# Sigmoid attention, routed experts and a SwiGLU-like layer on one core: operand pieces made inside the second layer and stored by the sync engine, first operands requested in tile 18, decodes and first casts at other places

## The chip, the cores and the metric

One core of one Trainium2 chip runs the whole kernel in one launch. The metric is the device time of one execution in microseconds (us); lower is better.

## The reference, cut to what matters

```python
scores = q @ k.T / sqrt(64) - log(448)            # 4 batches, 12 heads, 448 tokens
x = sigmoid(scores) @ v                           # -> 1792 tokens x 768
e = argmax(x @ w_gate)                            # one of 8 experts per token
y = gate * (relu(x @ w1[e]) @ w2[e])              # 768 -> 1024 -> 768
h = y @ w_in                                      # 768 -> 2048, w_in and w_out given as float64
out = (h * sigmoid(h)) @ w_out                    # 2048 -> 768
```

All results are float32. w_in and w_out arrive as 64-bit words, which the kernel turns into float32 itself.

## The kernel before

Every float32 matrix product is made of three products of rounded parts. An operand is cast to a high part (ScalarE, ACT) and the rest is subtracted out as a low part (VectorE, DVE); TensorE (PE) then adds high x high, high x low and low x high in PSUM. The names ending in h and l are those parts. The order on each engine is the order in which the code is written; each engine, and each queue that requests DMAs (that of the sync engine, SP, of ACT and of GpSimd, POOL), works strictly in that order.

**Stage 1, attention** (`scores`, `av`, `evac`, `xform`; steps k = 0 to 97, four per pair of heads, 24 pairs). `split_k` (in the first two steps of a pair) and `split_q` (in the last two) make the parts of the next pair's k and q. Beside it, `predecode` turns raw 64-bit words of w_in and of NO of the 16 w_out slabs into float32: `decode` is five DVE instructions of 128 x 768 with a yield after the second to fifth, `combine` forms the differences that the later seven-product scheme needs. The step loop draws from it with `next(pd, 0)`, six times in a pair. The last pair's loads, the first expert's weights and stores of decoded slabs leave from SP's queue.

**Stage 2, experts**: tiles t = 0 to 20 of 128 tokens sorted by expert. Some tiles from 7 to 13 are skipped by a branch. A tile is the first layer (`l1`, 36 matmuls of 128 x 512), `relu`, `htrans`, `xtrans` of the next tile, the second layer (`l2`, 48 matmuls of 128 x 384) and `yout` (ACT scales, SP stores to Yd). Where the next tile has another expert, a branch runs `split1` (six casts on ACT and six subtractions on DVE, of 128 x 1024) for its w1 and then loads the next; `split2` does so for w2, in the first layer and in the second. `early` decodes six more w_out slabs in tiles 1 and 2. In tile 0 the parts of w2 are made by `split2` in three calls.

**Between stages 2 and 3**, `xprep` makes the operands of the last layer: for a chunk c of 128 tokens it takes two gathered blocks of rows (`ra`, `rb`), transposes them in four groups of three (`tr`), forms sums and differences s1, s2, a21, s4, splits seven pieces into parts (`split(i, ...)`) and stores the 14 parts with `put` to T0 (first 1024 tokens, chunks 0 to 3, tiles 15 to 18) or T1 (other 768, chunks 0 to 2, in pass 0 of stage 3, `xprep1`). In stage 3 high parts, and the low parts of the first three pieces, lie in a ring of two buffers (tag `sl`), so a cast waits until an older part has landed in DRAM. `xload` brings the stored operands back: operands 0 and 1 are requested after tile 19, 2 to 4 in tile 20, 5 and 6 after it.

**Stage 3** (`ffn2`, pass 0 with 1024 tokens, pass 1 with 768; j = 0 to 7 in each). Each j makes seven products (63 matmuls of 128 x 512 in pass 0: the P phase), gates them (`gate`), and multiplies with w_out for the 8 (pass 1: 6) tiles of 128 tokens (96 or 72 matmuls of 128 x 384: the Y phase); DVE adds each tile to `acc`. Four PSUM buffers hold two tiles of y, so the third tile waits for the first tile's add. In pass 0 `bg(p)` draws one step of background work 12 times in a j, four of them in the P phase: first `wdecode`, the rest of w_out, one slab after the other through one raw buffer, then `xprep1`. In the last j of pass 0, between the P and the Y phase, these lines stand:

```python
if p == 0 and last:
    for _ in bgs:
        pass
    for i in range(7):
        xo[1][i] = xload(1, i)
```

Of the kernel before, what the change touches and what calls it, by code (L numbers as in the profile page):

```python
# [51 lines left out]
EARLY = {1: 3, 2: 3}  # L52
NO = 4
NM = NO + sum(EARLY.values())
# [12 lines left out]
def attn_moe_ffn(ctx: ExitStack, tc, qT, kT, v, wg, w1, w2, w_in, w_out, out):  # L67
# [604 lines left out]
    for k in range(0, G + LAG, 2):  # L672
# [25 lines left out]
        for j in (k, k + 1):  # L698
            background(j)
            if j >= 3:  # L700
                next(pd, 0)
                if j % 2:
                    next(pd, 0)
            if cur is None and j >= G - 8 and not tasks:
                cur = prep(0, (B - 1) * S)
                gg = gate(0, cur[1], (B - 1) * S)
            if j >= 4 * UG and j % 8 == 1 and TF + (j - 4 * UG) // 8 < TG:
                t = TF + (j - 4 * UG) // 8
                nc.sync.dma_start(out=Yd[t * 128:(t + 1) * 128], in_=zero)
# [37 lines left out]

    def split2(r, pool=(FC - 1,)):
        for k in r:
            nc.scalar.copy(out=w2h[:, k], in_=stage2[:, k])  # L750
            eng = nc.gpsimd if k in pool else nc.vector
            eng.tensor_sub(out=w2l[:, k], in0=stage2[:, k], in1=w2h[:, k])  # L752
# [54 lines left out]
    split2(range(0, 2), (1,))  # L807
    hs0 = relu(0, 0, ph0)
    until(x3, "pr")
    pn = counts()  # L810
# [6 lines left out]
    until(x3, "tt")  # L817
    split2(range(2, 4), (3,))
    nxt, nn = prep(1), prep(2)
# [8 lines left out]
    h1 = htrans(0, 1, hs1)  # L828
    split2(range(4, FC), (5, 7))
    until(tb, "ne")  # L830
# [18 lines left out]
    def xprep(p, c, ra, rb, tmp, slab, px, free=None):  # L849
# [4 lines left out]

        def put(i, ap, eng=nc.sync):
            eng.dma_start(out=td[i, :, :, cs], in_=ap.rearrange("p (k m) -> p k m", k=KH))

# [7 lines left out]
        def split(i, a, l=None):  # L865
            if free is None:
                h, s = slab()
                l = l if s is None else s
                nc.scalar.copy(out=h.bitcast(F32R), in_=a)
                nc.vector.tensor_sub(out=l.bitcast(F32R), in0=a, in1=h)  # L870
                put(2 * i, h, nc.scalar)
                put(2 * i + 1, l, nc.gpsimd)
                return
            h = slab()
            l = slab() if l is None else l
            nc.scalar.copy(out=h.bitcast(F32R), in_=a)
            put(2 * i, h)
            nc.vector.tensor_sub(out=l.bitcast(F32R), in0=a, in1=h)
            put(2 * i + 1, l)
# [63 lines left out]
    for t in range(TMAX):  # L943
# [10 lines left out]
        if t > 0:  # L954
# [23 lines left out]
            if t == TMAX - 1:  # L978
                M1.close()
                L0.close()  # L980
                F1 = Group("left")
                wp, xpa = F1.pool("f_w", 1), F1.pool("f_xa", 1)
                wiload(0)
                for i in (2, 3, 4):
                    xps[i] = xpa
                    xo[0][i] = xload(0, i)
                wops = [*wisplit()]
            l2(py, *h0, range(2, 4))
            l2(py, *h1, range(4, 8))
        if 0 < t and t + 1 < TMAX:  # L990
# [10 lines left out]
        yout(t, py, gg, tk)  # L1001
        if XPT <= t < XPT + NX:
            for _ in xg:
                pass
        if XPT - 1 <= t < XPT + NX - 1:
# [4 lines left out]
            if c == 0:  # L1010
# [6 lines left out]
                       (lambda it: lambda: next(it))(slabs), lambda i: keep(ps_t, [128, 384], F32, f"t{i}", 0))  # L1017
        if t == XPT + NX:
            for i in range(2):
# [46 lines left out]
    def wdecode():  # L1066
        raw = xs_t[:, 0:2 * DM].bitcast(I32).rearrange("p (n w) -> p n w", w=2)
        bt, sq = xs_t[:, 2 * DM:3 * DM].bitcast(I32), xs_t[:, 3 * DM:4 * DM]
        rawload(raw, w_out[:, NM], nc.sync)
        for f in range(NM, F2C):  # L1070
            yield 1
            yield 1
# [230 lines left out]
```

## Time and profile before

| | us |
|---|---|
| median of 3 runs (1079.37 to 1082.52) | 1081.44 |
| the profiled execution: time | 1077.8 |
| the profiled execution: span of the trace | 1076.1 |
| PE busy in the span | 1003.9 (93%) |
| DVE busy | 704.0 (65%) |
| ACT busy | 486.8 (45%) |
| POOL busy | 127.1 (12%) |

Times in the trace count from the start of the span. A busy PE is one on which a matmul is under way; it says nothing about the clock, which has a column of its own (1.00 is full speed).

### The profile page before, as it was taken

The page shows a single profiled execution, that of the slowest core. Times are in us where ns is not written, and L with a number is a line of the kernel's source. Part 1 is how long each engine was busy: PE and PEld are TensorE (multiplying, and loading weights), DVE is VectorE, ACT ScalarE, POOL GpSimd, SP SyncE. Part 2 cuts the span into 40 slices and gives each one's busy share as a digit, 9 for nine tenths or more (in the row PEclk, how much of TensorE's full clock was granted, in tenths as well). Part 3 has the DMA queues.
Part 4 walks back from the last instruction along what each step waited for, and adds up shares of the span by engine and source line. Part 5 has one row for each costly group of instructions (what it writes and reads, how often), then busy time and mean ns, then how long its engine had stood idle before and what let it go on. Part 6 is the DMA issues. An engine that isn't in the chain of part 4 may idle for free. (4 is left out here: it accounts for less than half of the span.)

```text
span 1076.1 us, 15547 instructions
## 1 busy us (share of the span) xinstructions
PE 1003.9 (93%) x5404; PEld 841.5 (78%) x5404; DVE 704.0 (65%) x1419; ACT 486.8 (45%) x823; POOL 127.1 (12%) x136
## 2 busy tenths in 40 slices
PE   7999998889999999898879879999999999999997
PEld 4555544579888998787768668898888899999997
DVE  5899994887775248363551337776876765777764
ACT  5666655421675246363442344322444336443342
POOL 1000000133122111224341000000000030000002
PEclk9999999999999999999989889999999999999999
DMA  8999999377698129597875933434454792222222
GB/s 287 332 328 316 323 311 272 122 248 257 251 344 324 33 89 357 175 329 207 266 262 188 416 133 125 169 125 134 127 176 159 263 380 83 81 82 82 81 81 89
DMA packets 83803, 226.12 MB, mean 210 GB/s; under 512 B 10176, under 2 KB 46528, under 8 KB 77696
## 3 DMA queue, kind: packets, MB, share of 16 engines
q1 hardware_dynamic: 63072, 188.02, 49.7%
q0 software_dynamic: 7584, 31.48, 8.7%
q10 hardware_dynamic: 13056, 5.51, 2.0%
q8 instruction: 44, 0.72, 0.3%
q14 instruction: 47, 0.39, 0.1%
HBM read 167.16 MB, written 57.82 MB: 209 GB/s over the span
## 5 line engine op out<-in xcount | busy, mean ns | idle before, releaser
L1197 PE MATMUL y<-wo,gl 128*128 128x384 f32 x448 | 151.6, 338 | 8.3 <-DVE gl L1130 8.3
L1195 PE MATMUL y<-wo,gh 128*128 128x384 f32 x448 | 152.1, 339 | 2.0 <-DVE acc L1206 2.0
L1196 PE MATMUL y<-wo,gh 128*128 128x384 f32 x448 | 150.6, 336 | 0.0
L1206 DVE TENSOR_TENSOR acc<-acc,y 128x384 f32<-128x384 f32 x196 | 101.3, 549 | 20.7 <-PE y L1197 20.4
L244 ACT ACTIVATE a<-s,bias 128x896 f32<-128x896 f32 x96 | 82.6, 911 | 68.5 <-PE s L241 68.4
L782 PE MATMUL y<-w2h,hh 128*128 128x384 f32 x304 | 105.6, 347 | 0.7 <-ACT hh L772 0.7
L783 PE MATMUL y<-w2l,hh 128*128 128x384 f32 x304 | 102.7, 338 | 3.3 <-POOL w2l L752 3.1
L784 PE MATMUL y<-w2h,hl 128*128 128x384 f32 x304 | 102.6, 337 | 0.9 <-DVE hl L773 0.9
L757 PE MATMUL h<-w1h,xh 128*128 128x512 f32 x228 | 93.8, 411 | 3.2 <-issue 2.0
L758 PE MATMUL h<-w1l,xh 128*128 128x512 f32 x228 | 92.7, 407 | 2.1 <-DVE w1l L746 1.5
L1197 PEld LDWEIGHTS y<-wo,gl 128*128 128x128 f32 x448 | 84.8, 189 | 10.3 <-DVE gl L1130 9.9
L759 PE MATMUL h<-w1h,xl 128*128 128x512 f32 x228 | 91.2, 400 | 0.0
L1195 PEld LDWEIGHTS y<-wo,gh 128*128 128x128 f32 x448 | 84.7, 189 | 4.7 <-DVE acc L1206 4.4
L1196 PEld LDWEIGHTS y<-wo,gh 128*128 128x128 f32 x448 | 84.7, 189 | 0.3
L773 DVE TENSOR_TENSOR hl<-x,hh 128x512 fp32r<-128x512 f32 x38 | 26.2, 689 | 89.0 <-ACT hh L772 66.2
L257 PE MATMUL o<-a,vf 128*64 128x448 f32 x384 | 84.0, 560 | 0.0
L935 DVE TENSOR_TENSOR wl<-wf,wh 128x384 fp32r<-128x384 f32 x112 | 60.7, 552 | 19.3 <-ACT wh L934 19.2
L1116 PE MATMUL X<-x,wh 128*128 128x512 f32 (+1 forms) x192 | 71.3, 371 | 1.3 <-ACT c L1156 1.3
L1117 PE MATMUL X<-x,wh 128*128 128x512 f32 (+1 forms) x192 | 70.3, 366 | 1.3 <-DMA x<-T 1.3
L1118 PE MATMUL X<-x,wl 128*128 128x512 f32 (+1 forms) x192 | 70.0, 365 | 0.0
L783 PEld LDWEIGHTS y<-w2l,hh 128*128 128x128 f32 x304 | 57.7, 190 | 4.0 <-POOL w2l L752 3.4
L1130 DVE TENSOR_TENSOR gl<-sg,gh 128x512 fp32r<-128x512 f32 (+1 forms) x64 | 40.0, 625 | 31.5 <-ACT gh L1128 30.4
(246 smaller groups left out, 2036.0 us busy)
## 6 DMA issues: line engine op xcount, KB each, us to landing
stage<-w SPq DMA_DIRECT2D x14, 1536.0 KB, 8.5
wf<-Wi SPq DMA_DIRECT2D x16, 1344.0 KB, 5.8
stage<-w SPq DMA_DIRECT2D x8, 1920.0 KB, 12.7
stage<-w_in SPq DMA_DIRECT2D x16, 768.0 KB, 6.4
wof<-Wo SPq DMA_DIRECT2D x16, 768.0 KB, 8.1
stage<-w SPq DMA_DIRECT2D x8, 1152.0 KB, 5.7
x<-T SPq DMA_DIRECT2D x12, 768.0 KB, 10.3
Yd<-ys SPq DMA_DIRECT2D x19, 384.5 KB, 4.7
```

The lines of the kernel that those rows point to most:

```text
L244: nc.scalar.activation(out=a[:, 0:n], in_=ps[:, 0:n, 0:S], func=AF.Sigmoid, bias=bias, scale=1.0 / math.sqrt(D))
L257: nc.tensor.matmul(out=po[pr][r, 0:S], lhsT=vf[:, g, r], rhs=a[:, i if n == 2 else 0], start=(g == 0), stop=(g == NG - 1))
L757: nc.tensor.matmul(out=ph, lhsT=xh[:, k], rhs=w1h[:, k, cs], start=(k == 0), stop=False)
L758: nc.tensor.matmul(out=ph, lhsT=xh[:, k], rhs=w1l[:, k, cs], start=False, stop=False)
L759: nc.tensor.matmul(out=ph, lhsT=xl[:, k], rhs=w1h[:, k, cs], start=False, stop=(k == KC - 1))
L782: nc.tensor.matmul(out=o, lhsT=hh[:, c], rhs=w2h[:, f, ys], start=(f == 0), stop=False)
L783: nc.tensor.matmul(out=o, lhsT=hh[:, c], rhs=w2l[:, f, ys], start=False, stop=False)
L784: nc.tensor.matmul(out=o, lhsT=hl[:, c], rhs=w2h[:, f, ys], start=False, stop=(f == FC - 1))
L1195: nc.tensor.matmul(out=o, lhsT=gh[:, cs], rhs=w_[:, f, 0, ys], start=st, stop=False)
L1196: nc.tensor.matmul(out=o, lhsT=gh[:, cs], rhs=w_[:, f, 1, ys], start=False, stop=False)
L1197: nc.tensor.matmul(out=o, lhsT=gl[:, cs], rhs=w_[:, f, 0, ys], start=False, stop=sp)
L1206: nc.vector.tensor_add(out=a, in0=a, in1=o)
```

## The change

`NO` falls from 4 to 2: two w_out slabs fewer are decoded in the attention stage and two more in pass 0, where `wdecode` now passes 13 steps before its first slab and takes six steps for a slab in place of seven. The steps that the attention loop draws are placed otherwise within a pair. In tile 0 the casts of w2 stand right after the first `relu`, and one subtraction goes from POOL to DVE. The four chunks of T0 are made between the matmuls of the second layer, not after the tile; all their stores leave from SP, and their last four subtractions go to POOL. `xload` of operands 0 and 1 stands after tile 18.

```diff
@@ -50,7 +50,7 @@
 KH = KC // 2
 HK = KH * 128
 EARLY = {1: 3, 2: 3}
-NO = 4
+NO = 2
 NM = NO + sum(EARLY.values())
 NL = TMAX - TMIN
 TF = TMIN - NL
@@ -699,7 +699,7 @@
             background(j)
             if j >= 3:
                 next(pd, 0)
-                if j % 2:
+                if j % NG >= 2:
                     next(pd, 0)
             if cur is None and j >= G - 8 and not tasks:
                 cur = prep(0, (B - 1) * S)
@@ -745,9 +745,10 @@
             nc.scalar.copy(out=w1h[:, k], in_=stage1[:, k])
             nc.vector.tensor_sub(out=w1l[:, k], in0=stage1[:, k], in1=w1h[:, k])
 
-    def split2(r, pool=(FC - 1,)):
+    def split2(r, pool=(FC - 1,), cast=True):
         for k in r:
-            nc.scalar.copy(out=w2h[:, k], in_=stage2[:, k])
+            if cast:
+                nc.scalar.copy(out=w2h[:, k], in_=stage2[:, k])
             eng = nc.gpsimd if k in pool else nc.vector
             eng.tensor_sub(out=w2l[:, k], in0=stage2[:, k], in1=w2h[:, k])
 
@@ -806,6 +807,8 @@
     l1(ph0, 0, *xhl, range(KC))
     split2(range(0, 2), (1,))
     hs0 = relu(0, 0, ph0)
+    for k in range(2, FC):
+        nc.scalar.copy(out=w2h[:, k], in_=stage2[:, k])
     until(x3, "pr")
     pn = counts()
     l1(ph1, 1, *xhl, range(KC))
@@ -815,7 +818,7 @@
     h0 = htrans(0, 0, hs0)
     hs1 = relu(0, 1, ph1)
     until(x3, "tt")
-    split2(range(2, 4), (3,))
+    split2(range(2, 4), (3,), False)
     nxt, nn = prep(1), prep(2)
     rawm = [ot_p[1].tile([128, DM, 2], I32, tag="ot", name="rawm0"),
             sqp[:, 0:2].rearrange("p n d -> p (n d)").bitcast(I32).rearrange("p (n w) -> p n w", w=2),
@@ -826,7 +829,7 @@
     py = psy(0)
     l2(py, *h0, range(0, 2))
     h1 = htrans(0, 1, hs1)
-    split2(range(4, FC), (5, 7))
+    split2(range(4, FC), (7,), False)
     until(tb, "ne")
     ne = ne1 = reg(tbl[0][0:1, 2, 0:1], (SP,), E - 1)
     nc.sync.dma_start(out=stage1, in_=wsrc(w1, ne, 0, KC))
@@ -852,8 +855,8 @@
         cs = slice(c * 128, (c + 1) * 128)
         td = T1 if p else T0
 
-        def put(i, ap, eng=nc.sync):
-            eng.dma_start(out=td[i, :, :, cs], in_=ap.rearrange("p (k m) -> p k m", k=KH))
+        def put(i, ap):
+            nc.sync.dma_start(out=td[i, :, :, cs], in_=ap.rearrange("p (k m) -> p k m", k=KH))
 
         def tr(rows, half, i):
             q = px(i)
@@ -865,11 +868,12 @@
         def split(i, a, l=None):
             if free is None:
                 h, s = slab()
+                eng = nc.gpsimd if s is None else nc.vector
                 l = l if s is None else s
                 nc.scalar.copy(out=h.bitcast(F32R), in_=a)
-                nc.vector.tensor_sub(out=l.bitcast(F32R), in0=a, in1=h)
-                put(2 * i, h, nc.scalar)
-                put(2 * i + 1, l, nc.gpsimd)
+                eng.tensor_sub(out=l.bitcast(F32R), in0=a, in1=h)
+                put(2 * i, h)
+                put(2 * i + 1, l)
                 return
             h = slab()
             l = slab() if l is None else l
@@ -985,8 +989,20 @@
                     xps[i] = xpa
                     xo[0][i] = xload(0, i)
                 wops = [*wisplit()]
+            px = xg if XPT <= t < XPT + NX else iter(())
+            next(px, 0)
+            next(px, 0)
             l2(py, *h0, range(2, 4))
-            l2(py, *h1, range(4, 8))
+            next(px, 0)
+            next(px, 0)
+            next(px, 0)
+            next(px, 0)
+            l2(py, *h1, range(4, 6))
+            next(px, 0)
+            next(px, 0)
+            l2(py, *h1, range(6, 8))
+            for _ in px:
+                pass
         if 0 < t and t + 1 < TMAX:
             i, c = entry(t + 1, late)
             fr = reg(tbl[i][0:1, 0, c], (ACT, DVE, SP, POOL), 1)
@@ -999,9 +1015,6 @@
         for _ in range(EARLY.get(t, 0)):
             early()
         yout(t, py, gg, tk)
-        if XPT <= t < XPT + NX:
-            for _ in xg:
-                pass
         if XPT - 1 <= t < XPT + NX - 1:
             c = t + 1 - XPT
             rows = ot_p[1].tile([128, 2, YW], F32, tag="ot", name=f"rows{c}")
@@ -1015,7 +1028,7 @@
                          [(sl8[:, 6], None), (sl8[:, 7], None), (rw[:, 0:HK], None), (rw[:, HK:2 * HK], None)])
             xg = xprep(0, c, rows[:, 0], rows[:, 1], [sl4[:, i] for i in range(4)],
                        (lambda it: lambda: next(it))(slabs), lambda i: keep(ps_t, [128, 384], F32, f"t{i}", 0))
-        if t == XPT + NX:
+        if t == XPT + NX - 1:
             for i in range(2):
                 xo[0][i] = xload(0, i)
         if t == 1:
@@ -1067,8 +1080,9 @@
         raw = xs_t[:, 0:2 * DM].bitcast(I32).rearrange("p (n w) -> p n w", w=2)
         bt, sq = xs_t[:, 2 * DM:3 * DM].bitcast(I32), xs_t[:, 3 * DM:4 * DM]
         rawload(raw, w_out[:, NM], nc.sync)
+        for _ in range(13):
+            yield 1
         for f in range(NM, F2C):
-            yield 1
             yield 1
             yield 1
             for i, _ in enumerate(decode(raw, sq, bt)):
```

Three places in the instruction order. First ACT in tile 17; `w2h` and `w1h` are expert weights, `t`, `sl`, `w` and `rows` hold xprep's pieces, `T` is the store to DRAM. Before:

```order
L750 CAST w2h<-stage_102 128x768 x3
L974 UNCONDITIONAL_BRANCH x2
L106 TENSOR_LOAD tbl_78
L994 COMPARE_AND_BRANCH
L745 CAST w1h<-stage_88 128x1024 x6
L994 UNCONDITIONAL_BRANCH x2
L795 ACTIVATE ys_2557<-y_2420,gg_2561 128x768
L885 COPY sl_5208<-t_0_2220 128x384
L869 CAST w_98<-t_0_2221 128x384
L856 DMA T_65<-w_98 384x1x128
L869 CAST w_98<-t_0_2220 128x384
L856 DMA T_65<-w_98 384x1x128
```

and after:

```order
L889 COPY sl_5194<-t_0_2206 128x384
L873 CAST w_98<-t_0_2207 128x384
L873 CAST w_98<-t_0_2206 128x384
L873 CAST w_98<-t_0_2207 128x384
L873 CAST w_98<-sl_5194 128x384 x2
L873 CAST rows_5650<-sl_5194 128x384 x2
L106 TENSOR_LOAD tbl_78
L1010 COMPARE_AND_BRANCH
L745 CAST w1h<-stage_88 128x1024 x6
L1010 UNCONDITIONAL_BRANCH x2
L796 ACTIVATE ys_2543<-y_2410,gg_2547 128x768
```

The pieces moved ahead of the six casts of w1 and of the output; the stores left ACT.

Second, POOL at the end of tile 16, where `rows` are the gathered rows of the next chunk, `gg` and `gx` gates and rows of coming tiles. Before:

```order
L856 DMA T_65<-w_98 384x1x128 x3
L856 DMA T_65<-sl_5208 384x1x128 x4
L843 DMA rows_5664<-Yd,cidx 128x769 x2
L590 DMA gg_2561<-Gd,gi_2400 128x1
L960 COMPARE_AND_BRANCH
L960 UNCONDITIONAL_BRANCH x2
L584 DMA gx_2402<-Xd,gi_2622 128x768
```

and after:

```order
L874 TENSOR_TENSOR sl_5194<-sl_5194,w_98 128x384 x2
L874 TENSOR_TENSOR sl_5194<-sl_5194,rows_5419 128x384 x2
L106 TENSOR_LOAD tbl_78
L1010 COMPARE_AND_BRANCH
L1010 UNCONDITIONAL_BRANCH x2
L846 DMA rows_5650<-Yd,cidx 128x769 x2
L590 DMA gg_2547<-Gd,gi_2390 128x1
L964 COMPARE_AND_BRANCH
L964 UNCONDITIONAL_BRANCH x2
L584 DMA gx_2392<-Xd,gi_2608 128x768
```

Seven stores on POOL became four subtractions, still ahead of the gathers.

Third, PE at the end of the P phase of the last j of pass 0 (X collects the last product, `ft` takes xprep1's transposes, y_7_4 is the Y phase's first tile). Before:

```order
L1116 MATMUL X<-x_6_6524,wh_6_8608 128x512
L1117 MATMUL X<-x_6_6524,wh_6_8608 128x512
L1118 MATMUL X<-x_6_6524,wl_6_8609 128x512
L1195 MATMUL y_7_4_0_8759<-wo_8643,gh_7_3_8698 128x384
L1196 MATMUL y_7_4_0_8759<-wo_8643,gh_7_3_8698 128x384
```

and after:

```order
L1130 MATMUL X<-x_6_6510,wh_6_8510 128x512
L1131 MATMUL X<-x_6_6510,wh_6_8510 128x512
L1132 MATMUL X<-x_6_6510,wl_6_8511 128x512
L864 MATMUL ft<-ident,xs_t 128x128 x12
L1209 MATMUL y_7_4_0_8759<-wo_8562,gh_7_3_8632 128x384
L1210 MATMUL y_7_4_0_8759<-wo_8562,gh_7_3_8632 128x384
```

Twelve transposes, a whole chunk of `xprep1`, now stand between the two phases. Before, the three chunks' transposes all stood in earlier phases.

## Rows read from the trace of the kernel before

**Rows 1.** The page, its first part: busy us, share, instructions of PE.

```profile
PE 1003.9 (93%) x5404; PEld 841.5 (78%) x5404; DVE 704.0 (65%) x1419; ACT 486.8 (45%) x823; POOL 127.1 (12%) x136
```

**Rows 2.** Waits of PE: releaser, us in total, times, longest.

```profile
PE x L769 <- ACT hs L763: 10.4, 5, 6.8
PE y L1197 <- DVE gl L1130: 8.3, 2, 7.7
PE s L241 <- DVE ql L223: 6.6, 10, 1.1
...
PE t L861 <- DVE sl L890: 4.3, 4, 1.6
PE t L861 <- ACT sl L885: 3.3, 4, 1.2
...
PE y L783 <- POOL w2l L752: 3.1, 1, 3.1
```

**Rows 3.** Stretches: length, busy us of each engine, PE's clock, DMA share, GB/s.

```profile
20.00:160.00 140.00, 133.38 (x817) 72.26 (x819) 127.39 (x316) 88.18 (x132) 0.00 (x0) 1.00 0.97 318
459.40:580.20 120.80, 103.23 (x540) 90.39 (x539) 60.08 (x113) 53.52 (x91) 41.68 (x46) 0.94 0.76 248
542.60:547.30 4.70, 4.70 (x13) 3.76 (x14) 1.66 (x3) 0.58 (x1) 3.62 (x3) 0.50 0.62 195
560.40:580.20 19.80, 18.53 (x101) 16.47 (x100) 6.92 (x14) 5.66 (x11) 6.65 (x9) 1.00 0.55 162
584.00:614.00 30.00, 25.55 (x123) 21.22 (x121) 8.70 (x15) 10.54 (x19) 0.00 (x0) 0.98 1.01 401
597.80:647.60 49.80, 36.82 (x161) 31.58 (x161) 19.70 (x34) 20.43 (x41) 0.00 (x0) 0.86 0.63 247
647.60:678.80 31.20, 31.20 (x161) 28.46 (x160) 25.09 (x45) 11.47 (x22) 0.00 (x0) 1.00 0.37 118
861.40:878.20 16.80, 16.80 (x98) 16.64 (x97) 12.99 (x26) 4.64 (x10) 7.39 (x7) 1.00 1.02 408
```

**Rows 4.** ACT in order of time: start, us, line, what, idle before and its releaser.

```profile
184.20 0.62 ACT L217 CAST kh<-kf 128x512 fp32r<-128x512 f32 x1 [3.93 <-DMA kf<-kT]
...
518.26 5.80 ACT L745 CAST w1h<-stage 128x1024 fp32r<-128x1024 f32 x6 [0.53 <-ACTq L974]
...
531.08 3.09 ACTq L856 DMA_DIRECT2D T<-w  x1
...
863.70 0.62 ACT L1128 CAST gh<-sg 128x512 fp32r<-128x512 f32 x1 [0.86 <-DVE sg L1127]
```

**Rows 5.** DVE in order of time.

```profile
48.08 0.96 DVE L123 SCALAR_TENSOR_TENSOR stage<-stage 128x768 int32<-128x768 int32 x1
...
301.20 2.21 DVE L746 TENSOR_TENSOR w1l<-stage,w1h 128x1024 fp32r<-128x1024 f32 x1 [0.59 <-DMA stage<-w]
...
519.34 6.90 DVE L746 TENSOR_TENSOR w1l<-stage,w1h 128x1024 fp32r<-128x1024 f32 x6 [0.89 <-DVEq L974]
...
626.91 0.56 DVE L113 TENSOR_SCALAR xs_t<-xs_t 128x768 int32<-128x768 int32 x1 [10.82 <-DMA xs_t<-w_out]
```

**Rows 6.** POOL in order of time.

```profile
222.06 3.62 POOL L752 TENSOR_TENSOR w2l<-stage,w2h 128x768 fp32r<-128x768 f32 x2
...
300.30 2.03 POOL L752 TENSOR_TENSOR w2l<-stage,w2h 128x768 fp32r<-128x768 f32 x1 [1.80 <-ACT w2h L750]
```

**Rows 7.** SP's queue: the requests of operands 2 to 4.

```profile
589.20 2.69 SPq L922 DMA_DIRECT2D x<-T  x6
```

**Rows 8.** Instructions on `sl`: duration ns min/median/max, first and last start.

```profile
L856 SPq DMA_DIRECT2D T<-sl x30: 512/521/618, 744.8 to 841.9; - x30
...
L876 ACT CAST sl<-ft x9: 472/473/482, 744.3 to 827.4; 128x384 fp32r<-128x384 f32 x9
L878 DVE TENSOR_TENSOR sl<-ft,sl x9: 548/551/559, 744.9 to 827.9; 128x384 fp32r<-128x384 f32 x9
...
DMA to landing us min/median/max: 2.3/2.3/2.4
```

## The prediction

> **What bounds the kernel now.** I read the page first. PE is busy for 1003.9 of 1076.1 us [rows 1], so at most some 72 us are to be had from waits, and what PE does at half clock on top. The reader should go next to PE's waits [rows 2] and ask where each lies, since only those beside moved code can change. Then come the windows [rows 3], which turn a stage into "length against the undisturbed length", the fairest measure of what a stage loses. ACT, DVE, POOL and SP in order of time [rows 4 to 7] say what the waited-for engine did before, and the view of one tile tag [rows 8] prices the store of a piece. Four places stand out: the attention, tiles 15 to 19, the first j of the last stage, and the end of pass 0, where today nothing is lost.
>
> **A, attention.** PE waits 6.6 us for `ql`, ten times up to 1.1 [rows 2]. `next(pd, 0)` draws a decode step of 0.96 us [rows 5]; of the two drawn at odd steps, one moves from ahead of `split_q` to behind it. About one step less ahead of each wait removes most of it: 5, bounds 2 and 6, because DVE is at 127.4 of 140 us here [rows 3] and could become the bound. Two slabs fewer also mean one 0.39 MB Wo store less ahead of the last pair's loads, at 318 GB/s [rows 3] 1.2 us of the 3.93 that ACT waits for `kf` [rows 4]. **A = -6.2** (2 to 10 gained).
>
> **B, tile 0.** PE waits 3.1 us for a `w2l` of POOL [rows 2], which made two of them at 1.81 us each [rows 6]. One goes to DVE and the casts come earlier, but POOL still makes one late in the row. **B = -2** (0 to 4).
>
> **D, tiles 15 to 19.** They take 120.8 us, PE busy for 103.2 [rows 3]; one tile is 18.5 us of PE at full clock. All `hs` waits of 10.4 and `sl` waits of 4.3 and 3.3 [rows 2] come from the pieces: after the tile ACT casts pieces, issues seven stores, one of which holds it for 3.09 us [rows 4], and so reaches the next tile's `relu` late. After the 6.8 wait PE's clock is 0.50 (1.2 GHz) for 4.7 us, half the work of that stretch [rows 3]. The change puts the pieces beside 48 matmuls of the second layer and takes the stores off ACT and POOL: all 18 us of waits go, and about 2.4 of half clock: 20.4.
>
> What comes instead is in tile 17. There `split1` follows, six casts of 5.80 and six subtractions of 6.90 [rows 4, 5], which today run in the second layer's shadow. After the change they stand behind eight piece operations on ACT, and behind DVE's. First-layer matmuls of tile 18 need `w1l` slab by slab; a slab comes every 1.15 (6.90/6), while PE uses one in 0.69 (three of 128x512, by the 31.20 us that 63 such and 96 of 128x384 take [rows 3]). I take 0.5 for DVE's end behind the second layer, 0.97 for the first cast, 1.15 for the first subtraction and 5 x (1.15 - 0.69) = 2.3: 4.9 us. POOL now subtracts four pieces just then. Before, one of DVE's 128x1024 subtractions took 2.21 instead of 1.15 and ended 1.08 after a POOL one that had begun 0.90 before it [rows 5, 6]. POOL takes 2.03 for 768 columns [rows 6], so 1.0 for 384; two of the four beside `w1l` add 1.9: 6.8 in all. (The Trainium skill, SBUF — State Buffer, section "SBUF: two separate sides", says why: VectorE with two SBUF inputs and a GpSimd operation that reads SBUF share a port pair under an exclusive lock, and the later one blocks for the whole instruction. By it all POOL subtractions delay DVE in full; without it the wait would stay 4.9. The row agrees.) A clock that halves again after such a wait costs about 1 more. The gathers of the next rows follow POOL's work and the landing of stores: 1 (0 to 2). **D = -20.4 + 8.8 = -12** (8 to 18).
>
> **E, the first j of pass 0.** It takes 49.8 us where the second takes 31.2, clock 0.86 [rows 3]: 18.6 lost. Seven operands of 1.57 MB each, 11 MB, start too late: DMA is saturated at 401 GB/s from 584 to 614 [rows 3]. Worse, DVE stands 10.82 us at its first decode, whose raw words come behind those loads in the queue [rows 5], and with it the `gl` that PE waits 7.7 for [rows 2]. Operands 0 and 1 (3.1 MB, 7.8 us of the queue) are now asked for a tile earlier, and the 13 new steps put the first decode into the second j, so the `gl` wait cannot occur there. What is left: from the request at 589.20 [rows 7] five operands and 1 MB of other loads (401 x 30 us = 12 MB, less 11) give 3.92 each: operand 5 lands at 607.4 + 2.3 = 609.7 and 6 at 613.6, while PE, 2.08 for each product of nine matmuls after 597.8, asks for them at 608.2 and, so delayed, at 611.8: 3.3 of waiting, 1 of clock. **E = -14** (9 to 18.6; the lower end is the gl wait and little else).
>
> **F, the end of pass 0**, the term that speaks against the change. `bg` draws 12 steps in a j, 88 before the loop `for _ in bgs` of the last j (7 x 12 + 4). Before, the steps were 42 of `wdecode` and 39 of `xprep1`, 81, all drawn by then. Now `wdecode` has 13 + 8 x 6 = 61; with 39 that is 100. The last 12 steps are exactly chunk 2, and run in a block between the P and the Y phase, which today follow each other without a gap: Y takes 16.8 us, PE busy for 16.8 [rows 3]. From P's end at 861.4: ACT still gates until 864.32, +2.9 [rows 4]. A part is cast (0.47) or subtracted (0.55), stored, and lands 2.3 after the issue [rows 8]; only two buffers hold high parts and the first three low ones. So casts that follow two buffers later wait for a landing. The fourth group of transposes needs the third's PSUM buffer read, which stands behind two such trips: PE is let go at +9.4. The rest of the pieces hold ACT to +17.2 and DVE to +17.8 (five landings in all in series, 5 x 2.3 = 11.5, and casts). Two y tiles run to +13.6 (2.1 each), the third waits for DVE's add to +18.3, and six more end at +30.9 against +16.8: 14.1. Half clock after two gaps of 9.4 and 4.7: 1.5. The loads of pass 1 move behind the block, 8.3 MB or 20 us from about +20, each just in time for its product. In the earlier j the missing chunk saves about what two more decodes take. **F = +15.6** (8, PE's bare block; 25, if the loads are late too).
>
> **Sum.** -6.2 - 2 - 12 - 14 + 15.6 = -18.6. On the profiled execution that is a span of 1057.5 and a time of 1059.2; that execution (1077.8) was 3.6 below the median of 1081.44, so the median becomes **1062.8**.
>
> **Rivals.** (1) The drain costs little, 5 or less, because the stores of the chunk overlap better than I chain them or because fewer steps are left: -29, **1052**. For it: the second buffer; against: the count of steps and the transposes, which the order shows. (2) Tile 17's queue eats D: `split1` behind the pieces, late gathers and the clock together cost 16 and not 9, D = -4.5: **1070**. For it: ACT, DVE and POOL all have work packed into the second layer; against: ACT is busy 53.5 of 120.8 and DVE 60.1 [rows 3]. (3) E stays bound by transfers: DMA is full for 30 us, and only 5 of 18.6 come back: **1072**. Against it: two of seven operands leave the crowd, and the first decode. (4) Slower: one mechanism, the ring in the drain. If a landing takes long there, since seven stores of a chunk, raw slabs and the loads meet in SP's queue and the Y stretch moves 408 GB/s [rows 3], five in series count fivefold. It decides at 2.3 + (18.6 + 3.2)/5 = 6.7 us each; at 8 each the time is 1062.8 + 28.5 = **1091**. Against: 30 landings of 2.3 to 2.4 so far [rows 8]. (5) The early request does not do what it says: the operands' loads wait on SP for chunk 3's last stores and move with the gathers, E = -5 and D a little less: **1074**. For a second view on the stores: the Trainium skill, DMA: Bandwidth & Descriptors, section "Issuing engines are not separate DMA queues", says that requesting from several engines saves only the issue time, usually small. By it stores moved off ACT would give back seven issues of 0.5 in a chunk; the row disagrees, for one issue alone held ACT for 3.09.
>
> **How the numbers follow.** Forecast 0.60, rival 1 0.13, rival 2 0.12, rival 3 0.08, rival 4 0.04, rival 5 0.03. The predicted time is the forecast's. Its terms' bounds taken together (half widths 4, 2, 5, 5 and 8, as squares) make 11 to either side: 1052 to 1074. That holds rivals 2, 3 and, at its edge, 1; I lower the low end to 1049 for the case that the drain is small and another term at its bound, and end at 1074; outside remain rival 4 and tails. About 0.3% (3.2 us; the three runs spread over 3.15) can be told from no change: faster 0.92; same 0.04, two of rivals 2, 3 and 5 at once; slower 0.04, rival 4.
>
> **What would show it.** In the changed kernel's profile: the `hs` and `sl` waits of PE gone and no store on ACT's queue (D); one stretch of PE waiting for DVE's `w1l` at tile 18, 5 to 7 us; the first j of pass 0 near 36 us, its waits all for operands 5 and 6 and none for `gl` (E); the last j's Y phase near 31 us, with twelve transposes in it and a wait of 4 to 5 for DVE behind its second tile (F); `ql` waits under 2 (A). The prediction fails if a stretch nobody touched grows, if the drain's length differs from +14 by more than 8, or if tile 18's wait is over 10.

## The result: 0.55% slower, and where the time went

The changed kernel takes 1085.75 us (median, 1079.36 to 1090.24) beside 1079.2 for the kernel before in the same comparison; the ratio is 1.0055, 95% interval 1.0038 to 1.0071. The forecast was 1062.8. It fell on the other side, through the place that rival 4 named (the end of pass 0), but for another reason than a slow ring.

The profiled execution took 1086.35 us, span 1084.7, 8.6 above the span of before. Since both kernels issue the same matmuls in nearly the same order, the plainest reading is the start of each phase on PE in the two traces, side by side; where their difference jumps, time was won or lost.

```
start of (us)                         before    after   after-before   step
first layer of tile 0                 200.73   188.50      -12.2       -12.2   A
first layer of tile 1                 229.52   218.86      -10.7        +1.6   B
second layer of tile 3                276.33   267.05       -9.3        +1.4
second layer of tile 15               468.75   459.65       -9.1        +0.2
first layer of tile 20                580.19   568.11      -12.1        -3.0   D
pass 0, P phase of j = 1              647.58   620.40      -27.2       -15.1   E
pass 0, P phase of j = 7              846.97   824.35      -22.6        +4.6
pass 1, Y phase of j = 0              889.60   895.31       +5.7       +28.3   F
end of the span                      1076.1   1084.7        +8.6        +2.9
```

The letters are the prediction's terms. E came as forecast, A larger; D gave a quarter of what it should, F cost nearly twice its term. PE's waits after (releaser, us in total, times, longest) answer to [rows 2]:

```profile
PE t L864 <- DMA rows<-Yd,cidx: 7.9, 3, 6.3
PE y L1211 <- DVE gl L1144: 6.8, 4, 2.7
PE ft L864 <- ACT xs_t L889: 5.4, 1, 5.4
PE s L241 <- DVE kh L217: 5.1, 1, 5.1
PE X L1131 <- DMA x<-T: 4.8, 3, 2.6
PE y L1209 <- DVE acc L1220: 3.8, 4, 2.6
PE h L759 <- DVE w1l L746: 3.8, 13, 1.0
PE s L241 <- DVE ql L223: 2.8, 3, 1.0
```

The old `hs` and `sl` waits are gone, as the change promised. New at the top are gathered rows (one wait of 6.3), the transposes of the drained chunk (`ft`, 5.4) and pass 1's operands. But waits alone don't add up to the loss: windows of after (length, busy us of PE, PEld, DVE, ACT, POOL, PE's clock, DMA share, GB/s) show what else there is.

```profile
459.70:568.10 108.40, 94.96 (x494) 83.58 (x493) 45.02 (x87) 45.20 (x81) 38.30 (x33) 0.94 0.82 262
585.70:620.40 34.70, 32.02 (x161) 28.36 (x160) 13.24 (x20) 18.73 (x36) 0.00 (x0) 1.00 0.66 262
824.30:839.00 14.70, 14.70 (x66) 11.73 (x65) 7.96 (x13) 7.11 (x13) 0.99 (x1) 1.00 0.89 306
839.00:851.50 12.50, 2.73 (x13) 1.75 (x12) 7.07 (x14) 3.87 (x8) 0.00 (x0) 0.66 0.29 87
851.50:873.40 21.90, 19.34 (x99) 19.02 (x98) 13.95 (x28) 5.42 (x12) 7.39 (x7) 0.88 0.82 275
873.40:895.30 21.90, 15.09 (x64) 12.95 (x64) 7.23 (x13) 6.00 (x11) 0.98 (x1) 0.84 1.02 418
```

Row 2 is j = 0 of pass 0: 34.7 in place of 49.8 [rows 3]. The last three rows are what stood as 16.8 us of undisturbed Y phase [rows 3], and the P phase behind it: a block of 12.5 in which PE works 2.7, a Y phase of 21.9 in place of 16.8 (half clock in part: 0.88), and a first P phase of pass 1 of 21.9 where before has 11.4 (length, busy, clock and DMA of before, next row).

```profile
878.20:889.60 11.40, 11.23 (x65) 10.91 (x64) 6.36 (x12) 5.31 (x10) 0.98 (x1) 1.00 0.78 281
```

So F is 12.5 + 5.1 + 10.5, and 0.3 in the P phase of j = 7. SP's queue of after shows the third part (start, us, line, what):

```profile
846.26 9.63 SPq L859 DMA_DIRECT2D T<-sl  x7
...
860.32 0.59 SPq L859 DMA_DIRECT2D T<-xs_t  x1
861.03 1.04 SPq L926 DMA_DIRECT2D x<-T  x2
...
863.34 18.59 SPq L926 DMA_DIRECT2D x<-T  x10
883.83 0.32 SPq L931 DMA_DIRECT2D wf<-Wi  x1
```

The operands of pass 1 are requested from 22.0 us after the end of the P phase (839.0) on, 12.4 before they are first used, and the last request leaves at 881.9. They are 8.3 MB; beside them go 3.1 MB of `out` (eight tiles of 0.39) and, requested last, 2.1 MB of the next weights. From 861.0 to 894.0, where PE's last wait for them ends, the DMA engines are at a full share and move 13.0 MB (395 GB/s).

### The profile page after: what moved, and what is told of

The parts are those of the page before. It is cut to its first block, busy times and chain, and to the rows that moved or that the text cites. A ratio compares the mean times of both kernels' runs of the same rounds, so it can differ in the third digit from the quotient of the medians.

```text
span 1084.7 us, 15559 instructions
## 1 busy us (share of the span) xinstructions
PE 1008.8 (93%) x5404; PEld 849.2 (78%) x5404; DVE 695.0 (64%) x1404; ACT 486.4 (45%) x823; POOL 122.9 (11%) x123
## 5 line engine op out<-in xcount | busy, mean ns | idle before, releaser
L1209 PEld LDWEIGHTS y<-wo,gh 128*128 128x128 f32 x448 | 86.0, 192 | 5.9 <-DVE acc L1220 5.4
L1210 PEld LDWEIGHTS y<-wo,gh 128*128 128x128 f32 x448 | 85.8, 191 | 0.2
L1158 ACT COPY c<-X 128x512 f32<-128x512 f32 (+1 forms) x16 | 8.5, 534 | 130.8 <-PE X L1132 130.8
```

Source lines behind the costliest of these rows:

```text
L1209: nc.tensor.matmul(out=o, lhsT=gh[:, cs], rhs=w_[:, f, 0, ys], start=st, stop=False)
L1210: nc.tensor.matmul(out=o, lhsT=gh[:, cs], rhs=w_[:, f, 1, ys], start=False, stop=False)
```

## The experiments

Theory after the result: F is the drain, and its unforeseen part is transfer time of late operands; D's shortfall is the gather of the next rows, which waits for stores that leave SP one after the other. Ratios below are to the kernel before, in each comparison.

**One idle step in place of 13**, so that nothing is left for the drain:

```diff
-        for _ in range(13):
+        for _ in range(1):
             yield 1
```

> The changed kernel with one idle step of wdecode in place of 13: 49 + 39 = 88 steps, so nothing is left for the drain in the last j of pass 0. Theory: the drain costs about 28 us in all (12.8 between the P and the Y phase, 5.1 more in the Y phase, 10.5 in the first P phase of pass 1, whose operands come late). Then 28 come back, less 3 to 8 where the first decode waits again for its raw words in j = 0: about 1058 to 1064, and the first P phase of pass 1 near 11.6 us. Rival: only the block between P and Y is the drain's, and the late operands of pass 1 have another cause (eight decodes and their stores in pass 0): about 1070, with that P phase still near 20 us.

1072.13 us, ratio 0.9951 (0.9932 to 0.9971): above both forecasts, and the first P phase of pass 1, 16.1, lies between them. Its windows say why: first j = 0, then the P and Y phase of j = 7 and the first P phase of pass 1.

```profile
585.10:630.30 45.20, 34.62 (x162) 30.61 (x161) 17.86 (x28) 18.66 (x36) 0.00 (x0) 0.89 0.59 228
833.40:847.90 14.50, 14.50 (x65) 11.80 (x65) 8.10 (x14) 7.28 (x13) 0.00 (x0) 1.00 0.76 255
847.90:866.70 18.80, 17.21 (x97) 16.44 (x96) 14.90 (x29) 5.27 (x11) 7.32 (x7) 1.00 0.95 349
866.70:882.80 16.10, 13.57 (x66) 12.17 (x65) 6.99 (x12) 5.76 (x11) 1.03 (x2) 0.89 1.02 421
```

The last three take 49.4, with the drain 71.0, before 42.6. So 21.6 came back; 6.8 remain, since the last chunk still ends only at the edge of the P phase, and pass 1's operands are requested behind it, from 849.0 on; the kernel before requests them from 2.3 us after the start of that phase. And j = 0 pays 10.5 (45.2 for 34.7): DVE is back in its wait for the raw words, which shows what the idle steps of the change are worth:

```profile
609.20 0.56 DVE L113 TENSOR_SCALAR xs_t<-xs_t 128x768 int32<-128x768 int32 x1 [10.52 <-DMA xs_t<-w_out]
```

**The kernel before with the drain alone.** 19 steps that do nothing, behind its own `wdecode`, push chunk 2 into the drain:

```diff
+    def idle():
+        for _ in range(19):
+            yield 1
-    bgs = chain(wdecode(), xprep1())
+    bgs = chain(wdecode(), idle(), xprep1())
```

> The kernel before with 19 idle steps between wdecode and xprep1, so that chunk 2 runs in the drain and nothing else is changed. Theory: +28 us over the kernel before, about 1107, with the same three parts (12.8, 5.1, 10.5). Rival, the prediction's term: +15.6, about 1095, the operands of pass 1 just in time.

1101.89 us, ratio 1.023 (1.020 to 1.026), 23.6 more than the median of before beside it (1078.27). The last windows, first the block, then the Y phase of j = 7 and the first P phase of pass 1:

```profile
857.70:870.10 12.40, 2.63 (x13) 1.65 (x11) 7.06 (x14) 3.75 (x8) 0.00 (x0) 0.63 0.29 88
870.10:892.30 22.20, 19.02 (x98) 18.70 (x97) 13.93 (x28) 5.43 (x12) 7.35 (x7) 0.90 0.80 266
892.30:914.00 21.70, 16.39 (x66) 14.10 (x65) 7.27 (x13) 6.02 (x11) 1.00 (x2) 0.76 1.02 418
```

12.4, 22.2 and 21.7: the drain's price is the same without any other part of the change, and the operands of pass 1 are late as in the theory, not in time as in the rival. From the P phase of j = 7 to the Y phase of pass 1 it takes 71.7 in place of 42.6, 29.1 more; j = 1 to 6, where chunk 2 no longer ran, take 195.6 in place of 199.4, which brings the total between the two forecasts.

**Half the bytes of pass 1's operands**, to separate a late request from a long transfer:

```diff
+        if p == 1:
+            hl = (hl[0], hl[0])
-        for h in range(2):
+        for h in range(2 - p):
```

> The changed kernel with its drain, but in pass 1 the low parts of the seven operands are not loaded (the high parts stand in for them): 4.1 MB in place of 8.3. Theory: the 10.5 us in the first P phase of pass 1 are transfer time of 8.3 MB beside 3.1 MB of stores of out: with half the bytes that phase falls from 22.1 to about 13, the total by 8 to 10 against the changed kernel, about 1077. Rival: the requests themselves come too late, whatever their size: the phase stays above 18, the total falls by at most 4.

Median 1074.46 us, ratio 0.9943 (0.9917 to 0.9969) against the changed kernel's 1.0055: about 12 us less. The one execution of it that was profiled took 2494.53 us, with PE busy in 99% of it; why is not known, and it says nothing of the phases. So the same kernel was profiled once more:

> The kernel with half of pass 1's operand bytes (low parts not loaded, high parts in their place) once more, for a profile of an ordinary execution. Theory: the first P phase of pass 1 near 13 us in place of 22.1, the 12.4 us block and the Y phase of 22 before it as they were. Rival: above 18.

```profile
821.90:848.50 26.60, 17.08 (x76) 13.34 (x75) 14.92 (x27) 10.98 (x20) 0.93 (x1) 0.88 0.62 209
848.50:872.00 23.50, 20.35 (x98) 20.02 (x97) 14.10 (x28) 5.42 (x12) 7.37 (x7) 0.85 0.84 284
872.00:883.40 11.40, 11.26 (x66) 10.94 (x65) 6.43 (x12) 5.31 (x10) 1.00 (x2) 1.00 1.01 418
```

1074.48 us. Block and Y phase are no shorter (the first row holds P phase and block), and the first P phase of pass 1 is back at 11.4. The requests begin as late as with the change (36.2 us after the start of the P phase of j = 7, there 36.7), they are half the bytes, and no wait is left: it is transfer time. The whole stretch takes 61.5 in place of 71.0, against 42.6 before; so of F's 28.3 some 9.4 are the transfer and 18.9 the drain itself.

**Six slabs in pass 0**, NO = 4 and 8 idle steps, 83 steps in all:

```diff
-NO = 2
+NO = 4
-        for _ in range(13):
+        for _ in range(8):
```

> The changed kernel with NO = 4 again (so only six slabs in pass 0) and 8 idle steps in place of 13: 8 + 36 + 39 = 83 steps, nothing left for the drain, and the first decode in the Y phase of j = 0, behind the landing of its raw words. Theory: the drain and the two more decodes are the whole loss of the last stage. The first j stays near 35 us, the stretch from the P phase of the last j to the Y phase of pass 1's first j falls from 71 to about 43, j = 1 to 6 give back some 4, the attention gives back 2 to 4 of its 12: about 1055 to 1060. Rival: the P phase of pass 1 stays late by 4 or more as with one idle step, and the total stays above 1063.

1074.63 us, ratio 0.9953 (0.9928 to 0.9978), a miss in the total, for a reason of its own: with the changed draws the fourth slab isn't finished in time, and its last decode step reads a buffer into which the first expert's weights are by then loaded (so part of w_out is not decoded here). DVE stands there:

```profile
170.87 0.96 DVE L123 SCALAR_TENSOR_TENSOR stage<-stage 128x768 int32<-128x768 int32 x1 [8.22 <-DMA stage<-w]
```

Tile 0 starts at 204.76, 16.3 later than after. What it was made for holds: from 840.75 to 883.40 it is 42.65, all of F's 28.3 gone, and j = 0 keeps its gain (599.61 to 635.21, 35.6).

**Eight slabs of five steps**, 5 idle steps, 84 in all:

```diff
-        for _ in range(13):
+        for _ in range(5):
             yield 1
         for f in range(NM, F2C):
             yield 1
-            yield 1
```

> The changed kernel with its eight slabs in pass 0, 5 idle steps and five steps for a slab in place of six: 5 + 40 + 39 = 84. The raw words of a slab are now asked for one step (about 2.2 us) nearer to their decode. Theory: as with NO = 4, but DVE waits some 2 us more for the raw words in each of eight slabs; where that falls into the P phase, PE waits for gl: 3 to 6 us in all, so about 1056 to 1062. Rival: DVE's waits hold every j's gl by their whole length, 15 us or more: above 1068.

1072.13 us, ratio 0.9906 (0.9872 to 0.9939). Windows: j = 0, j = 1 to 6, and the last three as above.

```profile
587.40:622.90 35.50, 31.91 (x160) 28.26 (x159) 16.47 (x25) 18.69 (x36) 0.00 (x0) 1.00 0.66 260
622.90:838.50 215.60, 199.34 (x992) 175.10 (x991) 159.00 (x288) 76.80 (x146) 6.65 (x6) 0.98 0.44 147
838.50:852.90 14.40, 14.40 (x64) 11.84 (x64) 8.14 (x13) 6.26 (x10) 0.00 (x0) 1.00 0.94 348
852.90:869.70 16.80, 16.80 (x98) 16.63 (x97) 13.00 (x26) 4.64 (x10) 7.38 (x7) 1.00 1.02 409
869.70:881.10 11.40, 11.23 (x64) 10.91 (x64) 6.37 (x12) 5.30 (x10) 0.98 (x1) 1.00 0.96 395
```

F and E are both whole. The price is in j = 1 to 6: 215.6, against 203.9 in the changed kernel and 199.4 in the one before. Beside the kernel with one idle step, which has the same eight slabs and takes 203.2, half of it lies in j = 1 to 3: j = 2 alone takes 40.6 in place of 33.6, since DVE waits 4.0 for raw words there and PE 3.4 behind it. The other half lies in j = 4 to 6: the chunks, of 12 steps in a j of 12, now begin with its first step, so that three of their four groups of transposes stand in the P phases, which take 16.6 to 17.3 there in place of 14.4. The change's 13 + 48 + 3 = 64 steps ahead of the first chunk put them into the Y phases. The total is the rival's, its mechanism is not: PE's waits for `gl` in j = 1 to 6 are 1.4 us in all.

**The gather of rows.** First only the order of the stores: pieces 2 and 3 instead of 4 and 6 use the rows' memory.

```diff
-[(sl8[:, 6], None), (sl8[:, 7], None), (rw[:, 0:HK], None), (rw[:, HK:2 * HK], None)]
+[(rw[:, 0:HK], None), (rw[:, HK:2 * HK], None), (sl8[:, 6], None), (sl8[:, 7], None)]
```

> The changed kernel, but pieces 2 and 3 (in place of 4 and 6) use the memory of the gathered rows, so that their stores leave four places earlier in SP's queue. Theory: in tile 16 PE waits 6.3 us for the gathered rows because the gather, into the same buffer, waits for the last of 14 stores that leave SP one in 0.69 us: four places earlier are 2.8 us, the wait falls to about 3.5 and the half clock behind it in part, 3 to 5 us in all, about 1082. Rival: the gather's own 6.9 us from issue to landing set the wait, or the stores begin late behind a load of weights on SP, and it stays within 1 us.

1080.64 us, ratio 1.0019 (1.0003 to 1.0035), as the theory has it. The wait fell to 4.4, and the second layer of tile 16 from 19.1 to 17.3; but kernels whose tile 16 is unchanged have 17.6 there (the one with one idle step) and a wait of 4.3 (the one with the old draws, below). Inconclusive alone. Then the cause itself was taken away, with another buffer:

```diff
+                rw = c2.tile([128, DM], F32, tag="xf", name="rw")
-            rw = rows.rearrange("p i w -> p (i w)")
```

> The changed kernel, but pieces 4 and 6 use a buffer of their own (128 x 768, free since the attention) in place of the gathered rows, so that the next chunk's gather, into the same rows, waits for no store. Theory: the 6.3 us wait of PE in tile 16 for gathered rows comes from that wait of the gather (8.48 us on POOL behind the last stores on SP); without it the gather is issued about 8 us earlier, right after POOL's subtractions, the three waits of 7.9 us in all fall under 1, and with the half clock behind them 8 to 10 us come back: ratio to the changed kernel about 0.992, some 1070 to 1073 beside a kernel before of 1078. Rival: the first half of the gather's delay is POOL's own order (it waits for PE's transposes, as where rows went first), and only 2 to 3 us come back.

1076.98 us, ratio 0.9958 (0.9934 to 0.9981). POOL of the changed kernel, and then of this one (start, us, what, idle before and its releaser):

```profile
482.81 1.02 POOL L846 DMA_INDIRECT rows<-Yd,cidx  x1 [8.48 <-DMA T<-rows]
```

```profile
472.99 1.99 POOL L874 TENSOR_TENSOR sl<-sl,rw 128x384 fp32r<-128x384 f32 x2
475.12 1.02 POOL L846 DMA_INDIRECT rows<-Yd,cidx  x1
```

The 8.48 us are gone, PE waits no more for rows, and from the second layer of tile 15 to tile 20 it is 10.6 us shorter (108.4 above; the six other profiles with that code have 105.4 to 108.9):

```profile
460.30:558.10 97.80, 92.31 (x495) 81.14 (x494) 44.76 (x87) 45.18 (x81) 39.17 (x33) 0.97 0.90 289
```

That is 13.6 under the 111.4 of the kernel before over the same tiles: the D that was forecast. Each measured against the kernel before, the one with the buffer has a ratio 0.0097 lower than the changed kernel, 10 us.

**The draws in the attention**, as before, with two slabs fewer:

```diff
-                if j % NG >= 2:
+                if j % 2:
```

> The changed kernel, but with the attention's draws as before (a second one at every odd step) and only the two slabs fewer. My step: the draws' place is worth 5 of the attention's 6.2, so the ql waits come back to near 6 us and the attention ends 4 to 5 later, near 186 + 5 = 191 us on the trace. Rival: what shortened the attention by 12 are the two slabs (10 decode steps on DVE, two stores), and it ends within 2 of 186 to 189.

1087.73 us, one execution. PE's `ql` waits are 4.9 in place of 2.8 (6.6 in [rows 2]), and tile 0 starts at 192.29. The nine other kernels with NO of 2 or 3 start it between 187.97 and 191.47, the two with the code of before at 200.73 and 197.19. So the draws' place is worth 1 to 4, and the two slabs 5 to 8, the most. The attention itself ends at 190.1, 3.8 later than with the change, as the theory has it, but also within 2 of the rival's 189: this one execution does not part the two forecasts.

**Tile 0's casts as before:**

```diff
-    for k in range(2, FC):
-        nc.scalar.copy(out=w2h[:, k], in_=stage2[:, k])
-    split2(range(2, 4), (3,), False)
+    split2(range(2, 4), (3,))
-    split2(range(4, FC), (7,), False)
+    split2(range(4, FC), (5, 7))
```

> The changed kernel with tile 0's casts and subtractions of w2 as before. Theory: the early casts moved PE's wait for w2l (3.1 to 0.9) into the first layer and the routing steps (xl 1.1, pb 1.2, and clock), so the stretch from the first layer of tile 0 to that of tile 1, 30.4 us with the change and 28.8 before, returns to about 28.8. Rival: it stays at 30 or above, since the routing on DVE, not the casts, sets it.

1087.92 us, one execution. From tile 0's first layer to tile 1's it takes 28.9, as the theory has it, with POOL's wait of 3.1 back. But the two kernels with 83 and 84 steps, whose tile 0 is the change's, also take 28.9, the others 29.6 to 30.9; and of the two with the code of before one takes 28.8 and one 31.1. What B costs, 0 to 2, stays within that scatter.

**Together:** the buffer for the pieces, NO = 3, and 7 idle steps, so that 52 steps stand ahead of the chunks (64 less one j of 12) and 88 in all.

```diff
-NO = 2
+NO = 3
-        for _ in range(13):
+        for _ in range(7):
+                rw = c2.tile([128, DM], F32, tag="xf", name="rw")
-            rw = rows.rearrange("p i w -> p (i w)")
```

> The changed kernel with the buffer of its own for pieces 4 and 6, NO = 3 (seven slabs in pass 0) and 7 idle steps: 7 + 42 + 39 = 88, nothing left for the drain, and the chunks begin at step 53, the fifth of a j, as in the changed kernel (65 there), so that their transposes fall into the Y phase. Theory: the gather's 9 to 10 us, the drain's 28 less the 6 to 7 that one idle step showed at the edge to pass 1, and the first j as in the changed kernel; the attention gives back some 3 for the third slab: 1085.75 - 10 - 22 + 3, about 1055 to 1060 (ratio to before about 0.98). Rival: the gains overlap or the first j loses again to the raw words: above 1066.

1057.08 us, ratio **0.9794** (0.9768 to 0.9819): faster than both kernels. Its windows: tiles 15 to 19, j = 0, j = 1 to 6, and the stretch of F in three.

```profile
459.50:557.30 97.80, 92.10 (x495) 81.14 (x494) 44.80 (x87) 45.16 (x81) 39.17 (x33) 0.97 0.90 289
574.90:610.00 35.10, 32.00 (x161) 28.33 (x160) 14.64 (x23) 18.69 (x36) 0.00 (x0) 1.00 0.65 260
610.00:813.80 203.80, 194.85 (x993) 173.63 (x992) 155.43 (x282) 74.69 (x142) 6.64 (x6) 1.00 0.43 144
813.80:828.20 14.40, 14.40 (x64) 11.73 (x64) 8.00 (x14) 7.28 (x13) 0.00 (x0) 1.00 0.77 256
828.20:847.10 18.90, 17.33 (x97) 16.54 (x97) 14.98 (x29) 5.27 (x11) 7.36 (x7) 1.00 0.94 345
847.10:864.20 17.10, 14.44 (x66) 13.86 (x65) 6.86 (x12) 5.30 (x10) 1.02 (x2) 0.80 1.02 420
```

The two repairs add up: 97.8 for D's tiles, 35.1 for E's first j, and 50.4 for the last three, which is 20.6 under the changed kernel and 7.8 over the one before. In the last row DMA is still full, at 420 GB/s.

The other way to save the slab, an early one in tile 3 with NO = 2:

```diff
-EARLY = {1: 3, 2: 3}
+EARLY = {1: 3, 2: 3, 3: 1}
-        for _ in range(13):
+        for _ in range(7):
+                rw = c2.tile([128, DM], F32, tag="xf", name="rw")
-            rw = rows.rearrange("p i w -> p (i w)")
```

> As with NO = 3, but NO stays 2 and the seventh early slab is decoded in tile 3. Theory: the attention keeps all its 12 us; a decode of 5 us in DVE in tile 3 costs 0 to 3: about 1053 to 1058, some 2 below the one with NO = 3. Rival: the decode holds w2's or hl's parts in tile 3 or 4 by its whole length, and it ends equal or above.

1061.73 us, ratio 0.9818 (0.9793 to 0.9842). From the first layer of tile 3 to that of tile 15 it takes 200.6 in place of 192.4, and 194.2 to 197.3 in the other changed kernels: the decode's 5 us on DVE cost 3 to 8, about their length, as the rival has it, and the attention gained nothing over NO = 3 (tile 0 starts at 189.49 and 189.99).

## Why the prediction was wrong, by its own steps

Term by term, the profiled execution misses the forecast by 27.3 us: A -6.0, B +3.6, D +9.0, E -1.1, F +12.7, the earlier j of pass 0 +4.6, the end of the program +2.9, and 1.6 in the tiles between B and D.

**F, the step that failed.** The count of steps, the twelve transposes in the drain and the wait behind the second y tile (2.6 where the text had 4.7) were right. Block and Y phase cost 17.6 more than before where the text had 15.6. The Y phase, put at "+30.9 against +16.8", ended at +34.4, because ACT gates until +5.4 and not +2.9 (843.76 + 0.62 against 839.0): casts of the chunk before (the last at 838.67) stand in this P phase ahead of the gates. In all ten traces with such casts the last gate ends 4.9 to 5.3 after P's last product, in the three without them 2.8. So the block is 12.5 where the text had PE let go at +9.4. The large miss is the sentence "8.3 MB or 20 us from about +20, each just in time for its product", which put the late loads at nothing: the requests began at +22.0, near that, but the same DMA engines also carried `out` and the next weights, 13.0 MB in 33 us, and PE lost 10.5. Half the bytes brought that phase back to its old length. That the drain could cost 25 with late loads stood in the bounds, not in the sum; 28.3 lies beyond even that.

**"In the earlier j the missing chunk saves about what two more decodes take."** It did not: +4.6 over j = 1 to 6, `gl` waits of 1.3 to 2.7 among them. The kernel before with the drain alone shows the chunk's saving by itself (3.8 us); so the new `wdecode` costs about 8.4. DVE waits six times for raw words in these j, 6.9 us in all, where the kernel before has no such wait, and three of the `gl` waits stand right behind. With seven slabs instead of eight the same j take 203.8, no less. That speaks for the raw words, which are asked for one step nearer to their decode, rather than for the number of slabs; no run has eight slabs of seven steps, so it isn't shown.

**D, the gathers of the next rows at "1 (0 to 2)".** This is the other step that failed, by some 10 us, as the separate buffer shows. The term named the landing of the stores, and both halves of its size stood in the text: the pieces begin a whole second layer earlier, and all 14 stores leave from one queue. They were never put side by side. SP issues one in 0.69 us, the last store of `rows` lands 8.5 after POOL is ready to gather, the gathers themselves take 6.9 to land, and the consumer is no longer behind the tile but some 9 us nearer. SP's queue in that tile, whose last pieces had been made by 474.3:

```profile
477.37 0.58 SPq L859 DMA_DIRECT2D T<-rows  x1
478.05 0.60 SPq L859 DMA_DIRECT2D T<-sl  x1
478.74 0.59 SPq L859 DMA_DIRECT2D T<-rows  x1
```

Rival 2 came near this size (D = -4.5 for the -3.0 measured) and names late gathers, but it put most of the loss on `split1`.

The other parts of D held: `hs` waits from 10.4 to 1.8, `sl` from 7.6 to 0.5. For `split1` in tile 17 the text had 6.8 of waiting; PE waited 1.4 for `w1h` and 2.1 for `w1l`, together about half of that. DVE's six subtractions took 8.60 beside POOL against 6.90 [rows 5]:

```profile
522.62 8.60 DVE L746 TENSOR_TENSOR w1l<-stage,w1h 128x1024 fp32r<-128x1024 f32 x6 [1.88 <-ACT w1h L745]
```

The 1.7 more is near the 1.9 put down for POOL's subtractions beside them; of these, the two that fell into that time took 3.94 in place of 1.99. The Trainium skill (SBUF — State Buffer, "SBUF: two separate sides") describes the port that the two engines share; the trace agrees.

**E** was right, in size (15.1 for 14) and mechanism: PE waits 1.3 each for operands 5 and 6 and not for `gl`, and both parts of the term were seen apart, since with one idle step the P phase kept its gain and the Y phase lost 10.4 again.

**A** was right in sign; 12.2 for 6.2. Some of that is luck: 3.5 is a stall of the one profiled execution of before (the 3.93 of ACT for `kf` in [rows 4], with PE standing 3.2 behind it), which the other trace with that code, with tile 0 at 197.19, does not have. The step that gives 5 to the draws looks wrong in its split, as far as one execution shows: the draws 1 to 4, the two slabs 5 to 8. **B** (-2) was +1.6 in the profile, within scatter. **The end** of the program took 2.8 to 3.1 more in each profile with the change, the outlying one aside, and in neither without it: after the last store SP waits 4.0 us for PE's sequencer, before 1.1. What holds PE there was not looked into, and stays open.

**Rival 4** named the right place and the right sign, but its mechanism is not what happened: the waits of ACT for landings in the drain are 2.5 and less, near the landings of [rows 8]. Rival 1, the drain costs little, has nothing left.

## What to carry to other kernels

When background work is drawn step by step, count the steps against the draws before anything else, and look which phase the remainder, and every chunk's first step, fall into; here twelve steps too many cost 28 us, and three chunks that fell into the P phases nearly 7. When a consumer is moved earlier, move its producer on paper too, with each store and request of the queue that the producer waits for. And a transfer is "just in time" only in a sum that holds all bytes of that stretch, not its own alone.

## What was not expected of the hardware

Stores of 192 KB left one queue one in 0.69 us, so that fourteen take 9.6 us to issue alone. The Trainium skill (DMA: Bandwidth & Descriptors, "Issuing engines are not separate DMA queues") calls the issue time usually small beside the transfer; here the queue's issue time, not a transfer, set when the last of them landed: the last store of `rows` left at 478.7, when its piece had been cast 7.9 us earlier. In the first P phase of pass 1 DMA carried 418 GB/s at a full share, against 281 in the same phase of the kernel before, so there was no slack to hide 5 MB in.
